# Two weight pieces loaded before the last table third, three converted before chunk 0, and most of a gate offset moved from products to transfers

## The chip, the core and the metric

The kernel runs on one core of one Trainium2 chip. TensorE (PE) multiplies, VectorE (DVE), ScalarE (ACT) and GpSimd (POOL) do the elementwise work, and SyncE (SP) issues nearly all transfers; each engine runs its own instructions in order. The metric is the device time of one execution in microseconds, the median of several runs.

## The reference

The input x has 8 batches of 3008 points with 256 features. It is transformed along both axes, the real part is kept, and every resulting row goes through a gated layer.

```python
X = np.fft.fft(np.fft.fft(x, axis=1), axis=2).real      # (8, 3008, 256)
x = X.reshape(24064, 256)
gate = 1.0 / (1.0 + np.exp(-(x @ w_gate)))              # w_gate, w_val: 256 x 1536
val = x @ w_val
out = gate * val @ w_out                                # w_out: 1536 x 256
```

The weights come in as 64-bit floats and are used as 32-bit ones.

## The kernel before

**Transform.** The points of a batch are folded on their symmetry, and the sums over points are matrix products with a table of cosines and one of sines (`stab`). Batch 0 is brought in by three thirds of x (`load_third`) and three thirds of each table (`load_table(t, j)`, two transfers each; t = 0 cosines, t = 1 sines). The results are `pk` (cosine side) and `qk` (sine side). The transform over features is merged into the weights: `merge` multiplies a converted piece of w_gate or w_val with the small table `dt`, and `merged` (ACT, L349) copies the result from PSUM into `G`. `G1` goes with pk, `G2` with qk.

**Weights.** There are 18 pieces (`jobs`): 0 to 11 are pieces of w_gate and w_val in turn, each for two column tiles f; 12 to 17 are pieces of w_out. A piece is loaded by SP (`weight_load`, 512 KB), split by two ACT activations (`weight_parts`, L301 and L302), put together by three DVE steps by way of a PSUM bank (`weight_join`, L313 to L316), and finished by an addition on POOL (L318). Then PE merges it (`weight_use`, tile name `ps`). Pieces 0 to 7 go through all this in the prologue, the others around the first steps of the main loop. The table of jobs and steps (`pre`, `mid`, `use`) says at which step i a piece's parts, join and use are placed.

**The offset ge.** One feature has no partner on the sine side. Its row `ek` times a number per column tile is written into PSUM ahead of the products, by `seed(i)` on ACT (L660, two activations with the scale `ge[:, g, f]`). `ge` is the first row of `G2`, turned so that each of 128 numbers lies on its own partition. `ge_sums` turns it on PE: a product of one row of G2 with a single 1.0 out of the tile `busy` for each column tile, and `ge_out` (ACT, L365) copies the column out of PSUM.

**Main loop.** A chunk is 252 output points. For every chunk the 12 column tiles f follow one another, one per step i. In a step PE does `front_a(i)` (G1 by pk, on top of the seed), then whatever weight work and products with the hidden layer are due, then `front_b(i)` (G2 by qk). Between the two, ACT keeps twice the first half (`part`, L671). One step later `gate_a` and `gate_b` make the gated values (ACT L685 and L699; DVE L686, L698 and L702). `seed(i + 1)` is given to ACT in step i, so column tile 4 is needed in step 3, tile 6 in step 5. From step 5 on, `back` multiplies the hidden layer with w_out: for the first chunk directly (`rows_start`, tile name `rows`), later by a scheme with fewer products (`po`).

**Banks.** Three PSUM banks (tag `x`) hold merges of the prologue and the seeded tiles `pf`. Five others (tags `po0` to `po4`) hold the sums of the sequence products, the joins and the ge products, and later the output sums.

**Order.** Each engine's order is the order of the calls. On SP, after the loads of pieces 0 to 7, x and the cosine table, come the three thirds of the sine table, pieces 8 to 13, then (when x is done with) pieces 14 to 17, the store of er to `ed`, and in the loop the rows `ek`, the mirror copies of later batches (`xr`) and the outputs. An SP transfer is not issued before the one eight places ahead of it has landed. The last sines (`sines(2)`) need the last third of the sine table.

Of the kernel before, what the change touches and what calls it, by code (L numbers as in the profile page):

```python
# [82 lines left out]
def kernel(  # L83
# [10 lines left out]
    nc = tc.nc  # L94
    B, _, _, _, D = xf.shape
    F = moe_w_gate.shape[1]
    P = 128
# [9 lines left out]
    NB = 1 + max(b // 3 for b in PLACE)  # L107
# [3 lines left out]
    N3 = NQ // 2  # L111
# [25 lines left out]
    def bank(name, other=None):  # L137
        if other is not None:
            return pso.tile([P, 512], F32, name=name, tag=f"po{other}")
        return psx.tile([P, 512], F32, name=name, tag="x")  # L140
# [45 lines left out]
    G1, G2 = G[:, 0], G[:, 1]  # L186
    ge = const.tile([P, 2, NFT], F32, name="ge")
# [8 lines left out]
    def load_table(t, j):  # L196
        q = slice(2 * j, 2 * j + 2)
        for rows in (slice(0, 112), slice(112, NP)):
            nc.sync.dma_start(out=ST[0][rows, t, q], in_=stab[rows, t, q])
# [48 lines left out]
    KEEP = 14  # L248

    def weight_load(j):  # L250


        w, c = jobs[j]
        src = (moe_w_gate, moe_w_val, moe_w_out)[w]
        src = src[2 * c * P : 2 * (c + 1) * P, :] if w == 2 else src[:, c * WC : (c + 1) * WC]
        src = src.rearrange("(c p) f -> p c f", p=P)

        def some(n, pool, tag):

            if tag not in shared:  # L260
                shared[tag] = pool.tile([P, n * WC], F32, name=f"w{tag}", tag=tag)
            return shared[tag]

        def home(j):

            if j in (0, 1, 2, 9):
                t = hp.tile([P, 6 * WC], F32, name="raw", tag="h")
                return t[:, 0 : 4 * WC], t[:, 4 * WC :]
            if j in (3, 4):
                ws = some(5, pqp, "qk")[:, (j - 3) * 2 * WC : (j - 2) * 2 * WC]  # L270
                return sp.tile([P, 4 * WC], F32, name="raw", tag="sf"), ws
            if j < 9:
                t = wf[:, (j - 4) % 4].rearrange("p m n -> p (m n)")
                return t[:, 0 : 4 * WC], t[:, 4 * WC : 6 * WC]
            if j < 12:
                shared[j] = cp.tile([P, 10 * WC], F32, name="wc", tag="c")
                return shared[j][:, 0 : 4 * WC], shared[j][:, 4 * WC : 6 * WC]
            return (shared[10][:, 6 * WC :] if j == 12 else shared["qk"][:, 0 : 4 * WC],
                    shared[11][:, (6 + 2 * (j - 12)) * WC : (8 + 2 * (j - 12)) * WC])

        if j < KEEP:
            raw, ws = home(j)
        else:
            both = some(24, xp, "x4").rearrange("p (i n) -> p i n", n=2 * WC)
            i = 3 * (j - KEEP)
            raw, ws = both[:, i : i + 2].rearrange("p a n -> p (a n)"), both[:, i + 2]
        raw = raw.bitcast(I32).rearrange("p (c f w) -> p c f w", c=2, w=2)
        ws = ws.rearrange("p (c f) -> p c f", c=2)
        WS[j] = ws
        if src.dtype == F32:  # L290
            nc.sync.dma_start(out=ws, in_=src)
        else:
            RAW[j] = raw
            nc.sync.dma_start(out=raw.rearrange("p c f w -> p c (f w)"), in_=src.bitcast(I32))  # L294

    def weight_parts(j):

        if j in RAW:
            raw, ws = RAW[j], WS[j]
            lo, hi = raw[:, :, :, 0], raw[:, :, :, 1]  # L300
            nc.scalar.activation(ws, hi.bitcast(F32), AF.Abs)  # L301
            nc.scalar.activation(lo, lo.bitcast(U32), AF.Copy, scale=2.0 ** -29)  # L302

    def weight_join(j, other=None):
        if j not in RAW:
            return
        raw, ws = RAW.pop(j), WS[j]
        lo, hi = raw[:, :, :, 0], raw[:, :, :, 1]
        wi = ws.bitcast(I32)
        mid_ = ws if other is None else bank("join", other).rearrange("p (c f) -> p c f", c=2)  # L310
        mi = mid_.bitcast(I32)
        ts = nc.vector.tensor_scalar
        ts(out=mid_, in0=ws, scalar1=2.0 ** -15, scalar2=HUGE, op0=ALU.max, op1=ALU.min)  # L313
        ts(out=mi, in0=mi, scalar1=3, scalar2=0x3FFFFFF8, op0=ALU.logical_shift_left,
           op1=ALU.bitwise_and)
        nc.vector.scalar_tensor_tensor(out=wi, in0=hi, scalar=-(2 ** 30), in1=mi,  # L316
                                       op0=ALU.bitwise_and, op1=ALU.bitwise_or)
        nc.gpsimd.tensor_tensor(wi, wi, lo, op=ALU.add)  # L318
# [25 lines left out]
    def merged(j):  # L344

        g, c = jobs[j]
        ps = MERGED.pop((g, c))
        cs = slice(c * WC, (c + 1) * WC)
        nc.scalar.copy(G[:, :, g, cs], ps.rearrange("p (h n) -> p h n", h=2))  # L349

    def ge_at(js):
        return [(jobs[j][0], f) for j in js for f in range(2 * jobs[j][1], 2 * jobs[j][1] + 2)]

    def ge_sums(js, other, ps=None):

        ps = bank("ge", other) if ps is None else ps
        for g, f in ge_at(js):
            mm(ps[:, g * NFT + f : g * NFT + f + 1], G2[0:1, g, f * P : (f + 1) * P], busy[0:1, 0:1],
               True, True)
        return ps  # L360

    def ge_out(js, ps):
        gs, fs = [sorted({a[i] for a in ge_at(js)}) for i in range(2)]
        to = slice(gs[0], gs[-1] + 1), slice(fs[0], fs[-1] + 1)
        nc.scalar.copy(ge[:, to[0], to[1]],  # L365
                       ps[:, 0 : 2 * NFT].rearrange("p (g f) -> p g f", g=2)[:, to[0], to[1]])
# [286 lines left out]
    def seed(i):  # L653

        _, _, n, f, _ = cut(i)
        PF[i] = bank("pf").rearrange("p (g n) -> p g n", g=2)[:, :, 0:n]
        for g in range(2):
            nc.scalar.activation(PF[i][:, g], EK[i // NFT], AF.Copy, scale=ge[:, g, f : f + 1])  # L660

    def front_a(i):
        (pk, *_), ks, _, _, fs = cut(i)
        for g in range(2):
            mm(PF[i][:, g], G1[:, g, fs], pk[:, ks], False, True)

    def part(i):

        pqe, ks, n, f, _ = cut(i)
        AP[i] = app.tile([P, 2, CH], F32, name="ae", tag="ae")[:, :, 0:n]  # L670
        nc.scalar.activation(AP[i], PF[i], AF.Copy, scale=2.0)  # L671
# [222 lines left out]
    ges = None  # L894
    for j in range(8):
        weight_parts(j)
        if j > 2:
            merged(j - 3)
        weight_join(j, j % 3)
        if j == 7:  # L900
            merged(5)
            ge_sums((4, 5), None, ges)
        weight_use(j)
        if 2 < j < 7:
            ges = ge_sums((j - 3,), 3, ges)
    ge_out(range(6), ges)
    for j in (6, 7):
        merged(j)
    for j in range(N3):
        load_table(1, j)  # L910
    for j in range(8, KEEP):
        weight_load(j)
    seq_start(0)
    folds = fold_ops(0, 2)
# [12 lines left out]
        for f in put:  # L927
            f(high)
    e0_spread()
    for i in range(N3):  # L930
        seed(i)
    for j in (8, 9):
        weight_parts(j)
    weight_join(8, NB - 1)
    sin = [seq_group(0, blk, 1, (2 * blk, 2 * blk + 1)) for blk in range(2)]

    def sines(j):
        for sums, _, _ in sin:
            sums(2 * j, 2 * j + 1)

    def first(i):
        front_a(i)
        if i < 2:
            part(i)
    sines(0)
    first(0)
    sines(1)
    first(1)
    sines(2)
    first(2)  # L950
    put = [then() for _, then, _ in sin]
    for high in range(2):
        for f in put:
            f(high)
    weight_join(9, NB - 1)
    for j in range(KEEP, len(jobs)):
        weight_load(j)
    nc.sync.dma_start(out=ed[0:1], in_=shared["er"])
    weight_parts(10)

    per = NFT * len(chunks)
    side = {}
# [5 lines left out]
    pre, use, mid = {}, {}, {}  # L968
    def using(j):
        weight_use(j, j % 2)  # L970
        if jobs[j][0] < 2:
            merged(j)
    for j, i in ((8, -2), (9, -1), (10, 0), (11, 1), (12, 2), (13, 4), (14, 6), (15, 8), (16, 10), (17, 12)):
        if i > 0:
            pre.setdefault(i - 1, []).append(lambda j=j: weight_parts(j))
        if i >= 0:
            mid.setdefault(i, []).append(lambda j=j: weight_join(j, 2))
        if jobs[j][0] == 2:
            use.setdefault(i + 2, []).append(lambda j=j: using(j))
    for j, i, other in ((8, 0, 3), (9, 2, 4), (10, 3, 3), (11, 4, 0)):  # L980
        use.setdefault(i, []).append(lambda j=j: using(j))
        use.setdefault(i + 1, []).append(lambda j=j, other=other: ge_out((j,), ge_sums((j,), other)))
    use[0].append(lambda: ge_out((6, 7), ge_sums((6, 7), 4)))


    i0 = NFT
# [123 lines left out]
```

## Time and profile before

| | us |
|---|---|
| median of 3 runs (lowest, highest) | 1935.59 (1934.75, 1937.33) |
| the profiled execution | 1937.33 |
| its span, first to last instruction | 1935.5 |
| PE busy | 1924.0 |
| POOL, DVE, ACT busy | 1561.6, 1435.0, 1346.7 |
| last sines on PE | 47.39 to 49.92 |
| first product of the hidden layer (rows) | 74.06 |
| ge products on PE (tile ge), before 39.7 and after 54.86 | 3.30 and 3.67 |

How to read it: the span is what the trace covers, and the time of an execution is 1.8 us more. Busy times of engines overlap. The mean granted clock of TensorE over the span is 0.998 of full speed. The stretch that the change touches ends at about 74 us; the rest of the span repeats chunks in which PE is busy nearly all the time.

### The profile page before, as it was taken

The numbers are of one execution on the slowest core, as the hardware profiler recorded it, in microseconds if no ns is written. First come the engines' busy times: TensorE is split into PE (matmuls) and PEld (weight loads), VectorE is DVE, ScalarE is ACT, GpSimd is POOL, SyncE is SP. The second block draws the span as 40 slices with busy tenths as digits, with TensorE's granted clock in tenths as the row PEclk, the third lists the DMA queues.
The fourth block names the chain that finished last, engine by engine and source line by source line (L and its number), as shares of the span: only waits on it lengthen the run. The fifth ranks groups of instructions, "written<-read, shape, count | busy, mean of one in ns | idle before, by whom it ended". The sixth has DMA issues, their size and how long they took to land.

```text
span 1935.5 us, 34483 instructions
## 1 busy us (share of the span) xinstructions
PE 1924.0 (99%) x11292; PEld 1793.3 (93%) x11292; DVE 1435.0 (74%) x3210; ACT 1346.7 (70%) x3152; POOL 1561.6 (81%) x2806
## 2 busy tenths in 40 slices
PE   9999999999999999999999999999999999999999
PEld 6899989999999999999999999999999999999998
DVE  7647887787777877777777776777777777776776
ACT  4777757767777677776777767777677766777775
POOL 2389988997889788987889879888789886777775
PEclk9999999999999999999999999999999999999999
DMA  9351421202022211312112021111200110011111
GB/s 289 124 111 36 107 79 47 58 17 79 15 56 51 63 31 20 77 24 80 19 42 60 14 83 24 47 47 24 83 14 15 22 20 14 15 20 22 25 17 30
DMA packets 165098, 97.87 MB, mean 51 GB/s; under 512 B 126298, under 2 KB 155068, under 8 KB 163128
## 3 DMA queue, kind: packets, MB, share of 16 engines
q1 hardware_dynamic: 164366, 95.17, 20.5%
q8 instruction: 91, 1.49, 0.3%
q14 instruction: 87, 0.71, 0.1%
q10 hardware_dynamic: 522, 0.50, 0.1%
q0 software_dynamic: 32, 0.00, 0.0%
HBM read 70.40 MB, written 47.24 MB: 61 GB/s over the span
## 4 chain that ended last, share of the span: by engine, by line
PE 94%; DVE 2%; DMA 2%; ACT 1%; SPq 0%; issue 0%; ACTq 0%; DVEq 0%
PE pf L135 49%; PE po L135 40%; PE ev L135 2%; PE rows L135 1%; DMA st<-in_stab_dram 1%; DVE c L826 1%; DMA raw<-in_moe_w_val_dram 1%; PE od L135 1%; DMA wf<-in_moe_w_val_dram 1%; DVE z L686 0%; PE ps L135 0%; PE row L135 0%; ACT pf L699 0%; DVE h L702 0%; DVE h L698 0%; SPq L294 0%
## 5 line engine op out<-in xcount | busy, mean ns | idle before, releaser
L708 POOL TENSOR_TENSOR sf<-h 128x168 f32<-128x168 f32 (+1 forms) x935 | 517.1, 572 | 215.9 <-DVE h L702 215.8
L708 POOL TENSOR_TENSOR sf<-h,sf 128x168 f32<-128x168 f32 (+1 forms) x1122 | 622.6, 574 | 57.5 <-DVE h L702 57.0
L135 PE MATMUL pf<-qk,G 128*128 128x252 f32 (+1 forms) x2304 | 584.3, 376 | 1.9 <-ACT ae L671 1.9
L135 PE MATMUL pf<-pk,G 128*128 128x252 f32 (+1 forms) x2304 | 582.9, 376 | 0.0
L702 DVE TENSOR_TENSOR h<-pf,z 128x252 f32<-128x252 f32 (+1 forms) x576 | 241.7, 420 | 425.7 <-ACT pf L699 425.7
L660 ACT ACTIVATE pf<-ek,ge 128x252 f32<-128x252 f32 (+1 forms) x1152 | 542.6, 471 | 19.3 <-DVE h L702 0.4
L135 PE MATMUL po<-sf,wf 128*128 128x168 f32 (+1 forms) x2992 | 516.2, 305 | 0.0
L671 ACT ACTIVATE ae<-pf 128x504 f32<-128x504 f32 (+1 forms) x576 | 339.0, 589 | 234.0 <-PE pf L135 231.8
L135 PEld LDWEIGHTS pf<-pk,G 128*128 128x128 f32 x2304 | 436.4, 190 | 53.3 <-issue 1.6
L135 PEld LDWEIGHTS po<-sf,wf 128*128 128x128 f32 x2992 | 460.5, 190 | 8.1
L135 PE MATMUL po<-h,wf 128*128 128x168 f32 (+1 forms) x2618 | 463.3, 305 | 0.0
L826 DVE TENSOR_TENSOR c<-c 128x168 f32<-128x168 f32 (+1 forms) x929 | 440.2, 506 | 5.1
L135 PEld LDWEIGHTS pf<-qk,G 128*128 128x128 f32 x2304 | 411.4, 190 | 29.7 <-ACT ae L671 3.1
L135 PEld LDWEIGHTS po<-h,wf 128*128 128x128 f32 x2618 | 416.5, 190 | 16.2
L686 DVE TENSOR_TENSOR z<-ae,pf 128x504 f32<-128x504 f32 (+1 forms) x576 | 383.7, 666 | 35.9 <-ACT h L685 34.4
L685 ACT ACTIVATE h<-pf 128x252 f32<-128x252 f32 (+1 forms) x576 | 217.7, 378 | 163.6 <-PE pf L135 158.2
L699 ACT ACTIVATE pf<-z 128x252 f32<-128x252 f32 (+1 forms) x576 | 214.0, 372 | 87.6 <-DVE h L698 85.2
L698 DVE TENSOR_TENSOR h<-h,pf 128x252 f32<-128x252 f32 (+1 forms) x576 | 233.0, 405 | 0.0
L708 POOL TENSOR_TENSOR sf<-sf 128x168 f32<-128x168 f32 (+1 forms) x187 | 107.2, 573 | 14.7
L708 POOL TENSOR_TENSOR sf<-sf,h 128x168 f32<-128x168 f32 (+1 forms) x187 | 101.7, 544 | 0.0
L739 ACT COPY c<-po 128x504 f32<-128x504 f32 (+1 forms) x141 | 80.0, 568 | 0.0
L835 DVE STREAM_TRANSPOSE os<-c 128x256 f32<-128x256 f32 x184 | 70.6, 421 | 0.3 <-issue 0.3
(152 smaller groups left out, 917.5 us busy)
## 6 DMA issues: line engine op xcount, KB each, us to landing
x<-xr SPq DMA_DIRECT2D x14, 1536.0 KB
out_dram<-os SPq DMA_DIRECT2D x368, 56.0 KB
xr<-in_xf_dram SPq DMA_DIRECT2D x14, 768.0 KB
xr<-in_xf_dram SPq DMA_DIRECT2D x35, 256.0 KB
ek<-ed SPq DMA_DIRECT2D x39, 126.0 KB
out_dram<-os SPq DMA_DIRECT2D x284, 7.0 KB
st<-in_stab_dram SPq DMA_DIRECT2D x6, 658.9 KB
x<-in_xf_dram SPq DMA_DIRECT2D x3, 1024.0 KB
```

The source lines that it names most:

```text
L135: nc.tensor.matmul(o, l, r, start=start, stop=stop, skip_group_check=True)
L660: nc.scalar.activation(PF[i][:, g], EK[i // NFT], AF.Copy, scale=ge[:, g, f : f + 1])
L671: nc.scalar.activation(AP[i], PF[i], AF.Copy, scale=2.0)
L685: nc.scalar.activation(H[p][:, fh, 0:n], PF[i][:, 0], AF.Sigmoid)
L686: nc.vector.tensor_tensor(z[:, :, ::-1], AP.pop(i), PF[i], op=ALU.subtract)
L698: nc.vector.tensor_tensor(h[:, fh, 0:n], h[:, fh, 0:n], pf[:, 1], op=ALU.mult)
L699: nc.scalar.activation(pf[:, 0], z[:, 0], AF.Sigmoid)
L702: nc.vector.tensor_tensor(h[:, fh, n:], pf[:, 0], z[:, 1], op=ALU.mult)
L708: nc.gpsimd.tensor_tensor(block(p, dst), block(p, a), block(p, b), op=(ALU.subtract, ALU.add)[op])
L739: (nc.vector.tensor_copy if t == 1 or t == 3 and not last else nc.scalar.copy)(C[0][:, 3 * t * R : 3 * (t + 1) * R], PO[t][:, 0 : 3 * R])
L826: engine.tensor_tensor(t[:, dst * R : (dst + 1) * R], *v, op=(ALU.subtract, ALU.add)[op])
L835: nc.vector.transpose(os_[0][:, s, 0:nb, h, :], t[:, c0 : c0 + nb * TB])
```

## The change

Four things are done.

1. SP loads pieces 8 and 9 ahead of the last third of the sine table, not behind it.
2. Pieces 8, 9 and 10 are split and joined before the last part of the sequence products is copied out: 8 and 9 between seed(0) and seed(1), 10 after the first sines and seed(2). Before, piece 8 was joined there and piece 9 just ahead of the loop. All three use bank po4. Piece 11 is split ahead of the loop and joined in step 0; before, this was piece 10, and 11 came in step 1.
3. Pieces 8, 9, 10 and 11 are merged in steps 0, 1, 2 and 3; before, in steps 0, 2, 3 and 4.
4. ge is made by products for pieces 0 to 3 alone. For pieces 4 to 11 each column tile is brought from G2's first row to the 128 partitions of ge by a transfer on SP (`ge_load`): 512 bytes each, two for a piece. The eight for pieces 4 to 7 stand behind the loads of pieces 14 to 17 and ahead of the store of er; the two for each of pieces 8 to 11 follow its merge. The copy of merge 5 into G moves behind merge 7.

```diff
+    def ge_load(j):
+        for g, f in ge_at((j,)):
+            nc.sync.dma_start(out=ge[:, g, f : f + 1], in_=G2[0:1, g, f * P : (f + 1) * P])
+
...
         weight_join(j, j % 3)
-        if j == 7:
-            merged(5)
-            ge_sums((4, 5), None, ges)
         weight_use(j)
-        if 2 < j < 7:
+        if j > 2 and j < 7:
             ges = ge_sums((j - 3,), 3, ges)
-    ge_out(range(6), ges)
-    for j in (6, 7):
+    ge_out(range(4), ges)
+    for j in (5, 6, 7):
         merged(j)
     for j in range(N3):
+        if j == N3 - 1:
+            weight_load(8)
+            weight_load(9)
         load_table(1, j)
-    for j in range(8, KEEP):
+    for j in range(10, KEEP):
         weight_load(j)
...
-    for i in range(N3):
-        seed(i)
+    seed(0)
     for j in (8, 9):
         weight_parts(j)
-    weight_join(8, NB - 1)
+        weight_join(j, NB - 1)
+    seed(1)
     sin = [seq_group(0, blk, 1, (2 * blk, 2 * blk + 1)) for blk in range(2)]
...
-    def first(i):
-        front_a(i)
-        if i < 2:
-            part(i)
-    sines(0)
-    first(0)
-    sines(1)
-    first(1)
-    sines(2)
-    first(2)
+    for j in range(N3):
+        sines(j)
+        front_a(j)
+        if j < 2:
+            part(j)
+        if not j:
+            seed(2)
+            weight_parts(10)
+            weight_join(10, NB - 1)
     put = [then() for _, then, _ in sin]
     for high in range(2):
         for f in put:
             f(high)
-    weight_join(9, NB - 1)
     for j in range(KEEP, len(jobs)):
         weight_load(j)
+    for j in range(4, 8):
+        ge_load(j)
     nc.sync.dma_start(out=ed[0:1], in_=shared["er"])
-    weight_parts(10)
+    weight_parts(11)
...
-    for j, i in ((8, -2), (9, -1), (10, 0), (11, 1), (12, 2), (13, 4), (14, 6), (15, 8), (16, 10), (17, 12)):
+    for j, i in ((11, 0), (12, 2), (13, 4), (14, 6), (15, 8), (16, 10), (17, 12)):
         if i > 0:
             pre.setdefault(i - 1, []).append(lambda j=j: weight_parts(j))
-        if i >= 0:
-            mid.setdefault(i, []).append(lambda j=j: weight_join(j, 2))
+        mid.setdefault(i, []).append(lambda j=j: weight_join(j, 2))
         if jobs[j][0] == 2:
             use.setdefault(i + 2, []).append(lambda j=j: using(j))
-    for j, i, other in ((8, 0, 3), (9, 2, 4), (10, 3, 3), (11, 4, 0)):
-        use.setdefault(i, []).append(lambda j=j: using(j))
-        use.setdefault(i + 1, []).append(lambda j=j, other=other: ge_out((j,), ge_sums((j,), other)))
-    use[0].append(lambda: ge_out((6, 7), ge_sums((6, 7), 4)))
+    for j in range(8, 12):
+        use.setdefault(j - 8, []).append(lambda j=j: (using(j), ge_load(j)))
```

## The prediction

> **What bounds the kernel now.** I read the busy times and the chain of waits on the page first, then the busy time by stage, the chain of the first 160 us, and the SyncE queue (SP).
>
> ```profile
> PE 1924.0 (99%) x11292; PEld 1793.3 (93%) x11292; DVE 1435.0 (74%) x3210; ACT 1346.7 (70%) x3152; POOL 1561.6 (81%) x2806
> ...
> PE 94%; DVE 2%; DMA 2%; ACT 1%; SPq 0%; issue 0%; ACTq 0%; DVEq 0%
> ```
>
> TensorE (PE) sets the end. The stages say where it is not at its best (columns: stretch, its length, then busy time and count on PE, PEld, DVE, ACT, POOL; granted clock, DMA share, GB/s):
>
> ```profile
> 39.70:50.92 11.22, 10.67 (x37) 6.64 (x36) 3.92 (x8) 7.28 (x16) 1.16 (x1) 1.00 1.02 307
> 53.10:57.06 3.96, 2.19 (x14) 1.81 (x14) 3.58 (x6) 0.90 (x3) 1.33 (x2) 1.00 1.05 393
> 57.06:63.80 6.74, 6.74 (x18) 5.52 (x19) 5.87 (x11) 4.55 (x11) 2.50 (x2) 0.50 0.08 28
> 74.06:1923.60 1849.54, 1847.53 (x10967) 1737.68 (x10967) 1375.48 (x3101) 1304.55 (x3066) 1537.89 (x2780) 1.00 0.19 43
> ```
>
> After 74 us PE idles 2 us in 1849, so a microsecond won or lost on PE's path before 74 us reaches the end whole. In 57.06:63.80 the granted clock is 0.50: the work took 6.74 us where full clock would take 3.37. It follows a stretch in which PE was busy 2.19 of 3.96 us, half of it single-column products. The chain names this work:
>
> ```profile
> 54.12 0.70 DVE raw L316
> 54.83 0.04 issue
> 54.87 1.05 PE ge L135 x8
> 55.91 1.05 PE pf L135 x4
> 56.96 0.81 PE ge L135 x4
> 57.78 1.98 PE pf L135 x4
> 59.76 3.41 PE ps L135 x8
> 63.17 2.12 PE pf L135 x8
> 65.29 0.53 PE ge L135 x4
> 65.82 1.92 PE ps L135 x8
> 67.74 1.70 PE pf L135 x8
> ```
>
> PE stood still until 54.87 for the last DVE step (L316) of converting piece 9, because ge (6, 7) shares its PSUM bank. Then ge lies between the products: 1.05 us for two pieces, 0.53 for one (two more follow, 69.44 and 73.60). Front products pf cost 0.85 a pair (1.70 for two), a merge (ps) 1.92.
>
> **Part 1: ge leaves PE.** After the last sines the loop loses ge for pieces 6 and 7 (1.05) and 8, 9, 10, 11 (4 x 0.53): 3.17 us at full clock. ge for 4 and 5, two pieces, leaves the prologue; there PE waits for DVE's folds and for the x transfer that ends DVE's wait at 32.02, so I take 0. The five small ACT copies (0.15 each) are off the path.
>
> **Part 2: the wait and the clock.** Nothing in chunk 0 shares a bank with a late conversion: the wait 53.10 to 54.87, 1.77 us, goes. Merge 8 started at 51.10, waiting for POOL; front_a(2) had ended about 50.77, so 0.33 goes. If the idle stretch goes, so should the half clock behind it: 6.74 - 3.37 = 3.37 us. Gains: 3.17 + 1.77 + 0.33 + 3.37 = 8.64.
>
> [...]
>
> **Part 3: two pieces ahead of the last table third.** ACT's conversions of 8 and 9 began as they landed:
>
> ```profile
> 46.78 0.67 ACT L301 ACTIVATE wf<-wf 128x512 f32<-128x512 f32 x1 [3.63 <-DMA wf<-in_moe_w_gate_dram]
> 48.20 0.68 ACT L301 ACTIVATE raw<-raw 128x512 f32<-128x512 f32 x1 [0.18 <-DMA raw<-in_moe_w_val_dram]
> ```
>
> So with the last table third ahead of them both were down by 48.2. Changed order, same bytes: that third lands by about 48.2, at most 48.9 (the second third had landed by 42.5, when the eighth issue behind it went out; 3.7 us for a third, two pieces of 1.35). Its sines ran from 47.39 without a wait; they now start between 48.2 and 48.9: +0.8 to +1.5, I take +1.1. ACT does parts 8, 9 ahead of seed(1), which ends near 47.4, so front_a(1) ends near 48.3, inside the same wait.
>
> The conversions cost nothing: DVE idles from 41.56 to 47.48 and takes joins 8 and 9 (three steps of 0.72) there. Piece 10 lands near 49.5 as before; ACT's parts(10) (1.25) precede part(1) and the two copies of the sines, DVE's join(10) (to about 52.4) precedes the first qk sums, done by 53.4. PE has front_a(2) from 51.0 and merge 8 from 51.9 to 53.8 as cover; without cover front_b(0) would wait at most 0.7. Join 11 (2.15) precedes gate_a(0) on DVE, and that cover holds too: front_a(3) at 61.0 needs seed(3) by 60; it can run at 58.4.
>
> Merges 9, 10, 11 now come one per step, i = 1, 2, 3, so step 4 has nothing between front_a(4) and front_b(4). part(4) on ACT took 0.59 after PE's matmuls had ended: PE idles 0.85 there. Costs: 1.1 + 0.85 = 1.95.
>
> **Part 4: sixteen small transfers on SP.** The first eight go behind pieces 14 to 17 and ahead of er's store; the rest follow merges 8 to 11, ahead of and behind chunk 1's ek row, all ahead of the mirror copies. Nothing among these is due before 80 us. What decides is when pieces 4 and 5 land: seed(4) needs them by 62.8 (front_a(4) at 63.8), seed(6) needs 6 and 7 by 68.8. SP reaches the first at about 53.3 (its last four loads were issued from 50.12 in 1.90 us, now 1.1 later). No transfer of 128 four-byte pieces into 128 partitions is in the trace. The neighbours:
>
> ```profile
> L649 SPq DMA_DIRECT2D ek<-ed x47: 338/344/2576, 74.2 to 1857.2; - x47
> ...
> L593 SPq DMA_DIRECT2D x<-in_xf_dram x7: 830/2146/9371, 103.6 to 136.1; - x7
> ...
> SPq L649 <- DMA ed<-er: 5.6, 1, 5.6
> ```
>
> Lower bound: ek's issue, 128 rows, 0.34 us. Upper bound: x8's (L593), 11.8 KB in 4-byte pieces, 3024 of them, 0.83 to 9.37. With 128 pieces ge is nearest ek: I take 0.4, four issued by 55, eight by 56.5 but for SP's waits for the transfer eight places back (a piece of a load each, the last landing near 59.5). The er store, issued at 52.12 at the end of the same queue of loads, landed 5.6 us after its issue, at 58.0; ge for 4 and 5 should land by 59 to 60, for 6 and 7 by 62. Both have room: 0.
>
> [...]
>
> **Sum.** 8.64 - 1.95 = 6.7 us. The profiled execution took 1937.33, its span 1935.5: the span should come to 1928.8 and that execution to 1930.6. The median of three, 1.74 below the profiled one, becomes 1935.59 - 6.7 = 1928.9. Stages that won't be shorter: DVE was busy 17.93 us between 50.92 and 74.06 and loses two joins (4.3), 13.6 left for a stage of some 16.4, so it doesn't become the bound.
>
> **Rivals.**
> A, the forecast: 1928.9, between 1927.0 (no cost at all, 8.64) and 1931 (waits for qk and the table at their upper bounds, 0.7 + 0.4, and a microsecond of unseen waits).
> B, the half clock stays or comes at another place: PE stands still for 1.1 us ahead of the last sines, and a gap of 1.77 was enough before. For it: one gap of like size did it. Against: around 41 us PE idled 0.55 us (two waits seen by PEld, 1.2) without a fall, and behind the new gap dense matmuls follow. It gives back 3.37: 1935.59 - 3.3 = 1932.3.
> C, ge's issue is as slow as x8's median, 2.15: the fourth lands at 53.3 + 8.6 + 0.5 = 62.4, just in time; the eighth at 71.0 for 68.8, so 2.2 are lost: 1931.1. Against: x8 has 24 times the pieces.
> D, the other side: SP serves the scattered transfers as it did x8's on average, (0.94 + 5.16 + 15.13) / 7 = 3.03 us. The fourth lands at 65.9, 3.1 late; the eighth at 78.0, when seed(6) would be due at 71.9: 6.1 more. PE stands idle in front_a(4) and front_a(6), which brings the half clock (3.37): -6.7 + 9.2 + 3.4 = +5.9, 1941.5. From 2.7 us an issue on it is slower without the clock (53.8 + 8 x 2.7 = 75.4, 6.6 past 68.8), from 2.3 with it. For it: elements of four bytes; against: their number.
> E, nothing reaches the end: some wait of chunk 0 that the present waits hide, such as ACT or DVE chains from seed to seed, takes all: 1935.6. Against: the stage's DVE and ACT have 2 us and more to spare.
>
> **How the numbers follow.** A 0.64, B 0.12, C 0.10, D 0.11, E 0.03. About 0.2% (3.9 us) can be told from no change: faster is A, C and a quarter of B, 0.77; same the rest of B and E, 0.12; slower D, 0.11. The range takes A, B, C: 1926.5 (the no-cost bound less half a microsecond of spread) to 1933.5 (B and a microsecond), with 0.86.
>
> **What would show it.** No ge on PE after 30 us; granted clock 1.00 from 10 to 1900 us; the last sines starting at 48.2 to 48.9 behind a wait for the table; merges 8 to 11 within 52 to 63; the first rows product at about 67.2 instead of 74.06; ACT's seeds (L660) with no wait for a DMA. The forecast is wrong if seed(4) or seed(6) waits for ge's transfers, if the sines wait beyond 49, if the clock shows 0.5 between 47 and 67, or if PE idles by more than 3 us in all between 51 and 68.

## The result, and the profile after

| | before | after |
|---|---|---|
| median of 18 runs each (lowest, highest) | 1935.66 (1934.05, 1938.08) | 1931.72 (1928.27, 1933.60) |
| ratio, 95% interval | | 0.9977 (0.997 to 0.9984) |
| the profiled execution | 1937.33 | 1931.39 |
| its span | 1935.5 | 1929.5 |
| start of front_a(2) on PE | 49.92 | 50.85 |
| first product of the hidden layer (rows) | 74.06 | 68.25 |
| from there to the end of the span | 1861.4 | 1861.25 |

The kernel became 3.9 us faster by the medians (3.1 to 5.8 by the interval); 6.7 had been forecast. The last line says where to look: once the rows products begin, both kernels take the same time, so all is decided ahead of it, in the first 74 us.

Busy times and the chain of waits on the page of the changed kernel:

```profile
PE 1916.0 (99%) x11260; PEld 1786.7 (93%) x11260; DVE 1433.5 (74%) x3210; ACT 1346.7 (70%) x3147; POOL 1562.0 (81%) x2806
...
PE 94%; DVE 3%; DMA 2%; ACT 1%; issue 0%; SPq 0%; ACTq 0%; DVEq 0%
```

PE has 32 matmuls fewer (16 pairs of ge) and 8.0 us less to do, of which 3.37 had been half clock. The same by stage (stretch, its length, busy time and count on PE, PEld, DVE, ACT, POOL, granted clock, DMA share, GB/s):

```profile
38.89:50.85 11.96, 9.94 (x34) 6.00 (x33) 6.86 (x12) 7.99 (x17) 2.58 (x2) 1.00 1.04 299
50.85:68.25 17.40, 15.26 (x69) 12.59 (x68) 13.21 (x25) 13.24 (x30) 3.88 (x3) 1.00 0.49 140
68.25:1918.00 1849.75, 1847.74 (x10969) 1737.81 (x10968) 1376.20 (x3106) 1305.93 (x3066) 1539.61 (x2781) 1.00 0.19 43
```

The stretch from front_a(2) to the first rows shrank from 24.14 (49.92 to 74.06) to 17.40 us, at full clock throughout; PE still idles 17.40 - 15.26 = 2.14 us in it. The stretch of the sequence products ahead of it has 2.02 us of idle PE (11.96 - 9.94) where before's had 0.55. PE's timeline of the changed kernel shows both (start, length, instruction; in brackets the idle time just before it and what ended it):

```profile
47.36 1.12 PE L135 MATMUL pf<-pk,G 128*128 128x252 f32 x4 [1.47 <-ACT pf L664]
48.31 0.80 PE L135 MATMUL ev<-st,x 126*128 126x377 f32 x2
...
50.85 1.01 PE L135 MATMUL pf<-pk,G 128*128 128x252 f32 x4
51.70 1.89 PE L135 MATMUL ps<-wf,dt 128*128 128x256 f32 x8
53.43 1.01 PE L135 MATMUL pf<-qk,G 128*128 128x252 f32 x4
...
60.17 1.12 PE L135 MATMUL pf<-pk,G 128*128 128x252 f32 x4 [0.57 <-ACT pf L664]
...
66.42 1.12 PE L135 MATMUL pf<-qk,G 128*128 128x252 f32 x4 [1.56 <-ACT ae L675]
67.38 1.04 PE L135 MATMUL pf<-pk,G 128*128 128x252 f32 x4
```

Behind 47 us three waits are left, all for ACT: front_a(1) for seed(1) (1.47), front_a(3) for seed(3) (0.57), front_b(4) for part(4) (1.56); the other 0.55 ahead of 50.85, for DVE, was there before too. 0.57 + 1.56 = 2.13 is all of the idle time behind 50.85. ACT's timeline says why (seed, part and the sigmoids stand in lines L664, L675 and L689 of the changed kernel):

```profile
45.21 0.67 ACT L301 ACTIVATE raw<-raw 128x512 f32<-128x512 f32 x1 [1.56 <-DMA raw<-in_moe_w_val_dram]
45.79 0.66 ACT L302 ACTIVATE raw<-raw 128x512 int32<-128x512 uint32 x1
46.34 0.97 ACT L664 ACTIVATE pf<-ek,ge 128x252 f32<-128x252 f32 x2
...
63.94 0.66 ACT L301 ACTIVATE wc<-wqk 128x512 f32<-128x512 f32 x1
64.51 0.64 ACT L302 ACTIVATE wqk<-wqk 128x512 int32<-128x512 uint32 x1
65.05 0.56 ACT L349 COPY G<-ps 128x512 f32<-128x512 f32 x1
65.51 0.38 ACT L689 ACTIVATE h<-pf 128x252 f32<-128x252 f32 x1
65.79 0.58 ACT L675 ACTIVATE ae<-pf 128x504 f32<-128x504 f32 x1
```

seed(1) (46.34) is queued behind the split of piece 9, which waited for its load. part(4) (65.79) is queued behind the split of piece 13, the copy of merge 11 and a sigmoid of gate 3: it starts 1.2 us after PE's four products from 63.74 (about 0.85 of work) have ended, where I had counted on its own 0.59 alone.

The chain of work that ended last holds no PE between 49.8 and 66.4 us. It runs through DVE and ACT: joins 10, 11 and 12, the splits of pieces 12 and 13 and the gates are its main links. The part around join 12 and seed(4) (start, length, engine, what):

```profile
60.28 0.62 DVE join L313
60.90 0.02 issue
60.92 0.71 DVE join L314
61.63 0.02 issue
61.66 0.69 DVE wc L316
62.34 0.34 DVE h L706
62.69 0.02 issue
62.71 0.48 ACT pf L664
```

So chunk 0 is now set by the order of DVE's and ACT's work, though each of the two is busy only 13.2 of its 17.40 us.

SP's timeline, and its group of ge transfers (least, median and greatest time of one issue in ns):

```profile
53.05 7.64 SPq L364 DMA_DIRECT2D ge<-G  x8
60.79 0.40 SPq L962 DMA_DIRECT2D ed<-er  x1
61.28 2.42 SPq L364 DMA_DIRECT2D ge<-G  x4
...
L364 SPq DMA_DIRECT2D ge<-G x16: 469/548/612, 53.0 to 66.2; - x16
```

A ge transfer took 0.55 us to issue (0.4 assumed); the first eight were out by 60.7, with 3.0 us of that spent in three waits for loads eight places back. No seed waited for a transfer: the waits of L664 are two, both for DVE, 1.1 us in all.

### The profile page after: what moved, and what is told of

The parts are those of the page before. It is cut to its first block, busy times and chain, and to the rows that moved or that the text cites. A ratio compares the mean times of both kernels' runs of the same rounds, so it can differ in the third digit from the quotient of the medians.

```text
span 1929.5 us, 34456 instructions
## 1 busy us (share of the span) xinstructions
PE 1916.0 (99%) x11260; PEld 1786.7 (93%) x11260; DVE 1433.5 (74%) x3210; ACT 1346.7 (70%) x3147; POOL 1562.0 (81%) x2806
## 4 chain that ended last, share of the span: by engine, by line
PE 94%; DVE 3%; DMA 2%; ACT 1%; issue 0%; SPq 0%; ACTq 0%; DVEq 0%
PE pf L135 49%; PE po L135 40%; PE ev L135 2%; DMA st<-in_stab_dram 2%; PE rows L135 1%; DVE c L830 1%; DMA wc<-in_moe_w_gate_dram 1%; PE od L135 1%; DVE z L690 0%; ACT pf L703 0%; PE row L135 0%; DMA raw<-in_moe_w_val_dram 0%; DVE h L706 0%; DVE h L702 0%; ACT ae L675 0%
## 5 line engine op out<-in xcount | busy, mean ns | idle before, releaser
L664 ACT ACTIVATE pf<-ek,ge 128x252 f32<-128x252 f32 (+1 forms) x1152 | 543.0, 471 | 20.0 <-DVE h L706 1.1
L675 ACT ACTIVATE ae<-pf 128x504 f32<-128x504 f32 (+1 forms) x576 | 339.6, 590 | 232.5 <-PE pf L135 229.3
L689 ACT ACTIVATE h<-pf 128x252 f32<-128x252 f32 (+1 forms) x576 | 218.1, 379 | 161.6 <-PE pf L135 156.9
```

The source lines that it names most:

```text
L689: nc.scalar.activation(H[p][:, fh, 0:n], PF[i][:, 0], AF.Sigmoid)
```

## Experiments

Twelve runs, in sessions of up to four on one chip. "Before" is the median of the kernel before in the same session.

| | edit | median | before | ratio (95%) |
|---|---|---|---|---|
| b_again | before, again | 1936.05 | 1935.78 | 1.0 (0.9991 to 1.0009) |
| a_again | after, again | 1930.25 | 1935.78 | 0.9969 (0.9956 to 0.9981) |
| b_fill | before + dense products where PE waits | 1935.39 | 1935.78 | 0.9997 (0.9988 to 1.0005) |
| b_ge | before + ge transfers alone | 1931.86 | 1935.78 | 0.9978 (0.9968 to 0.9987) |
| a_prod | after, ge of 4 to 11 by products | 1934.85 | 1935.55 | 0.9995 (0.9986 to 1.0004) |
| a_seeds | after, seeds first on ACT | 1932.55 | 1935.55 | 0.9982 (0.9973 to 0.9991) |
| a_late13 | after, piece 13 a step later | 1931.33 | 1935.55 | 0.9977 (0.9968 to 0.9986) |
| a_both | the two edits above | 1931.09 | 1935.55 | 0.9978 (0.997 to 0.9987) |
| c_load | after, seeds first, old order of loads | 1932.33 | 1936.36 | 0.9981 (0.9972 to 0.9989) |
| c_cand | the same, pieces placed anew | 1932.77 | 1936.36 | 0.9983 (0.9974 to 0.9992) |
| a_again2 | after, third time | 1930.66 | 1935.62 | 0.9974 (0.9963 to 0.9985) |
| a_late13_2 | a_late13 again | 1930.78 | 1935.62 | 0.9971 (0.9961 to 0.9982) |

**b_again: the kernel before, unchanged**, for a second trace of it.

> The kernel before once more, for a second trace of it and its spread. Theory (the 3.37 us of half clock were in the profiled execution and not in every one): ratio 1.000, and a span 1 to 3 us under 1935.5 with a shorter half-clock stretch or none. Rival (half clock is in every execution and the shortfall lies in the changed kernel alone): again 6 to 7 us at 0.50 behind the wait for piece 9, span 1935 or more.

In this execution there was no half clock. PE's timeline of it:

```profile
53.19 1.05 PE L135 MATMUL ge<-busy,G 1*128 1x1 f32 x8 [1.16 <-DVE raw L316]
...
60.58 1.12 PE L135 MATMUL pf<-pk,G 128*128 128x252 f32 x4 [1.13 <-ACT pf L660]
```

The wait for the bank is there, 1.16 instead of 1.77. The second line is new: at full clock PE comes to front_a(3) before ACT has written seed(3). In the first profile the half clock covered this wait. From front_a(2) to rows it took 21.28 us (49.29 to 70.57) against 24.14: 2.86 less, of which 0.61 is the shorter wait for the bank and 3.37 - 1.13 = 2.24 what the half clock cost net, by these two traces.

The runs of the kernel before in all sessions here, this one included, give the size: of 102 whose granted clock was listed, 62 had a mean clock of 0.998 or less and took 1936.65 us on average, 40 had 0.999 or more and took 1934.71. I read the lower mean clock as the half clock of the first trace: 3.37 us lost in 1935.5 make a mean of 0.998. It is then in some six of ten executions and costs 1.9 us there, so 62 / 102 x 1.94 = 1.2 on average. Where in an execution the clock fell is seen in the traces alone.

**a_again: the changed kernel, unchanged.**

> The changed kernel once more. Theory (its cost is the order of ACT's work, the same in each execution): waits of PE again at front_a(1) (1.5 us), front_a(3) (0.6) and front_b(4) (1.6), span within 1 us of 1929.5, 3 to 5 us under the kernel before. Rival (landing of transfers varies and sets the time): other waits, at the sines or at the seeds for a DMA, and a span that moves by 2 us or more with them.

The same three waits: 1.42, 0.67 and 1.56; 17.49 us from front_a(2) to rows. The span, 1930.8, is 1.3 longer than the first one, and the gain in the time, 5.5, is more than was expected; PE also waited 1.62 for a third of the cosine table here, so the rival is right in part. This and a_again2 have 12 runs, all at a clock of 0.999 or more, and of the 18 runs of the result one is at 0.998 (the slowest, 1933.60): the half clock of the old place did not come back.

**b_fill: does the idle stretch cause the half clock?** Four dense products, whose result nothing uses, stand in the kernel before where PE waits for the bank.

```diff
+    def fill(n):
+        ps = bank("fill", 1)
+        for _ in range(n):
+            mm(ps[:, 0:CH], busy[:, 0:P], busy, True, True)
+    use[0].append(lambda: fill(4))
```

> The kernel before, with four dense products into a free bank where PE waits for piece 9's conversion (their output is not used). Theory (the idle and thin stretch lets the clock fall): the clock stays at 1.00 from 57 to 64 us and the time falls by what the half clock costs on average, 1.5 to 3.4 us. Rival (the clock falls for another reason, or seldom): no change within 1 us, or slower by up to 1.7 us if the fill itself is in the way.

All 11 runs had a mean clock of 1.000, against 40 of 102 at 0.999 or more without the fill. PE by stage from front_a(2) on, first the kernel with the fill, then b_again over the like stretch:

```profile
49.38:53.40 4.02, 4.02 (x20) 3.58 (x19) 3.62 (x7) 3.36 (x7) 0.56 (x1) 1.00 0.73 218
```

```profile
49.29:53.19 3.90, 2.74 (x13) 2.09 (x12) 3.50 (x7) 2.90 (x6) 0.00 (x0) 1.00 0.83 253
```

PE is busy all of 4.02 us, where it was busy 2.74 of 3.90. So the idle stretch is the cause here, and with dense work in it none of the 11 runs shows the fall. The time did not fall by the 1.5 to 3.4 that the theory named (1935.39; the interval takes in no change): the ge products came 0.56 later (53.75 against 53.19), seed(3) was waited for as before (1.13), and 1.2 us was all there was to win on average; 0.56 of it went to the fill itself.

**b_ge: the ge transfers (the fourth item of the change) alone.** The kernel before with ge of pieces 4 to 11 by transfers, its order of loads and conversions kept.

```diff
-        if j == 7:
-            merged(5)
-            ge_sums((4, 5), None, ges)
...
+    for j in range(4, 8):
+        ge_load(j)
...
-    for j, i, other in ((8, 0, 3), (9, 2, 4), (10, 3, 3), (11, 4, 0)):
-        use.setdefault(i, []).append(lambda j=j: using(j))
-        use.setdefault(i + 1, []).append(lambda j=j, other=other: ge_out((j,), ge_sums((j,), other)))
-    use[0].append(lambda: ge_out((6, 7), ge_sums((6, 7), 4)))
+    for j, i in ((8, 0), (9, 2), (10, 3), (11, 4)):
+        use.setdefault(i, []).append(lambda j=j: (using(j), ge_load(j)))
```

> The kernel before with ge of pieces 4 to 11 by transfers and nothing else changed: loads, conversions and merges stay in the old order. Theory (ge's products, the wait for the shared bank and the clock are the gain, the new order of loads and conversions costs): 5 to 7 us under the kernel before, so 1 to 3 under the changed one. Rival (the new order is what pays, or the transfers cost on SP): 3 us or less under the kernel before.

It gained 3.9 us, less than expected and as much as the whole change in the result. What the first three items bring on top can hardly be seen: 0.8 us by the means (1931.88 over 9 runs, 1931.06 over the 30 of the changed kernel), with an uncertainty as large; beside it on the same chip, a_again's five runs were 1.6 us faster by the medians. PE's timeline and a window of it:

```profile
55.43 1.99 PE L135 MATMUL ps<-raw,dt 128*128 128x256 f32 x8 [0.97 <-POOL raw L318]
60.31 1.80 PE L135 MATMUL pf<-pk,G 128*128 128x252 f32 x4 [1.99 <-ACT pf L664]
```

```profile
60.00:63.00 3.00, 2.69 (x7) 2.23 (x8) 2.93 (x6) 2.22 (x6) 0.98 (x2) 0.60 0.18 34
```

Without the ge products the wait for the bank is gone, but two others took its place: merge 9 waits for POOL's last step of piece 9 (0.97), front_a(3) for seed(3) (1.99), and behind that the clock falls to 0.60 over 60 to 63. DVE, busy 2.93 of these 3 us, had joins 9 to 12 in this stage.

**a_prod: the order alone.** The changed kernel with ge of pieces 4 to 11 made by products again, on banks po3 and po4, so that none shares one with a late conversion.

```diff
-    for j in range(4, 8):
-        ge_load(j)
...
-        use.setdefault(j - 8, []).append(lambda j=j: (using(j), ge_load(j)))
+        use.setdefault(j - 8, []).append(lambda j=j: using(j))
+    for j, other in ((8, 3), (9, 4), (10, 3), (11, 4)):
+        use.setdefault(j - 7, []).append(lambda j=j, other=other: ge_out((j,), ge_sums((j,), other)))
+    use[0].append(lambda: ge_out((6, 7), ge_sums((6, 7), 4)))
```

> The changed kernel with ge of pieces 4 to 11 by products again (banks po3 and po4 in turn, each one step after its merge); loads, conversions and merges in the new order. Theory (the transfers carry the gain, the new order alone little): 2 to 3.5 us slower than the changed kernel, 1 to 2 under the kernel before. Rival (the new order carries the gain): within 1 us of the changed kernel.

It is 0.7 us faster than before, which can't be told from nothing, and some 3.4 slower than the changed kernel (1934.85 against a pooled median of 1931.4). From front_a(2) to rows, by stage:

```profile
52.46:71.35 18.89, 18.74 (x94) 15.45 (x92) 13.75 (x26) 13.83 (x35) 3.89 (x3) 1.00 0.33 119
```

PE is full: 18.74 us of 18.89, against 15.26 with the transfers, and 18.74 - 15.26 = 3.48 is what the ge products cost (3.17 in the sum). The stretch is 2.4 us shorter than in b_again, but it starts at 52.46, 3.2 later: in these traces, what the order wins behind the sines it gives back ahead of them. With the ge products on it PE, idle for 0.15 us of that stretch, sets chunk 0; without them it is idle for 2.14, for ACT, and the chain runs through DVE and ACT.

**a_seeds: who makes front_a(1) late?** The changed kernel with the three seeds ahead of the splits of pieces 8 and 9 on ACT.

```diff
-    seed(0)
+    for i in range(N3):
+        seed(i)
     for j in (8, 9):
         weight_parts(j)
         weight_join(j, NB - 1)
-    seed(1)
```

> The changed kernel with the three seeds ahead of the conversions on ACT, as before the change. Theory (PE's 1.5 us wait ahead of front_a(1) is ACT's order: seed(1) behind piece 9's landing and split): front_a(1) without a wait, the last sines waiting for the table instead by 0 to 1, 0.5 to 1.5 us faster than the changed kernel. Rival (the table lands no earlier than seed(1) is ready): the same wait of 1.5 us moves to the last sines, no change in time.

The wait of front_a(1) went, and the time did not follow. PE's timeline, and its window behind:

```profile
48.57 0.92 PE L135 MATMUL ev<-st,x 126*128 126x377 f32 x2 [2.68 <-DMA st<-in_stab_dram]
```

```profile
48.00:52.00 4.00, 3.43 (x7) 2.03 (x8) 2.02 (x4) 2.05 (x4) 1.28 (x1) 0.66 0.47 173
```

Between 36 us and front_a(2) PE now waits once, for the last table third (2.68), and the clock falls to 0.66 behind it. The rival was right: here the table is the later of the two, and seed(1) only stood in front of it. Piece 10, next in the queue behind the table, landed 1.0 us after it (49.60 against 48.57). In the profile of the changed kernel piece 10 was there at 49.11, which puts the table at about 48.1 as an estimate, 0.2 ahead of the last sines: without the wait for seed(1) they would hardly have started sooner.

**a_late13: part(4) behind piece 13.** The changed kernel with piece 13 split in step 4 and joined in step 5.

```diff
-    for j, i in ((11, 0), (12, 2), (13, 4), (14, 6), (15, 8), (16, 10), (17, 12)):
+    for j, i in ((11, 0), (12, 2), (13, 5), (14, 6), (15, 8), (16, 10), (17, 12)):
```

> The changed kernel with piece 13 split, joined and used one step later (step 5 in place of 4). Theory (front_b(4) waits 1.6 us because part(4) stands behind piece 13's two activations on ACT): that wait falls to 0.7, 0.7 to 1 us faster than the changed kernel. Rival (part(4) waits for the gates of step 3, on DVE): no change.

PE's timeline:

```profile
63.03 1.12 PE L135 MATMUL pf<-qk,G 128*128 128x252 f32 x4 [0.68 <-ACT ae L675]
```

The wait fell from 1.56 to 0.68, and front_a(2) to rows from 17.40 to 16.56. In the time, 1931.33, nothing shows: 0.9 us is less than what front_a(2)'s start moves from trace to trace (48.30 here, 50.85 in the first).

**a_both: the two edits together.**

> Seeds first and piece 13 a step later in one kernel. Theory (two separate waits on PE's path): the gains add, 1.2 to 2.5 us faster than the changed kernel, 5.5 to 7 under the kernel before. Rival (the second wait takes up what the first gives): no more than the better of the two alone.

A miss: the chunk took 16.68 us, with the 0.68 again, but the median is 1931.09, no better than piece 13's move alone. In its profiled execution PE stood still earlier, for a third of the cosine table, which the change does not touch:

```profile
37.41 0.81 PE L135 MATMUL pe<-st,x 126*1 126x377 f32 x8 [3.34 <-DMA st<-in_stab_dram]
```

**c_load: does the new order of loads earn anything?** a_seeds with pieces 8 and 9 loaded behind the last table third again.

```diff
-        if j == N3 - 1:
-            weight_load(8)
-            weight_load(9)
         load_table(1, j)
-    for j in range(10, KEEP):
+    for j in range(8, KEEP):
```

> The changed kernel with seeds first and pieces 8 and 9 loaded behind the last table third, as before the change; conversions still all ahead of the sine sums' copies. Theory (the new load order costs about 2 us at the last sines, but the early conversions need it): front_a(2) starts near 49.7 as in the kernel before, the qk sums come about 2 us later behind joins 9 and 10, front_b(0) waits 1 to 2 us, and the time is within 1 us of the changed kernel. Rival (the load order costs without need): 1.5 us or more faster than the changed kernel.

PE's timeline:

```profile
54.29 1.12 PE L135 MATMUL pf<-qk,G 128*128 128x252 f32 x4 [1.19 <-DVE qk L537]
```

front_a(2) starts at 49.84, early as expected, but the joins now stand on DVE ahead of the qk sums, and front_b(0) waits 1.19 for them; rows begin at 69.60. Against the kernel before of its own session c_load gains 4.0 us and a_seeds 3.0: the two orders are worth the same within about a microsecond.

**c_cand: the old order of loads, with the pieces placed to fit.** Loads and seeds are as in c_load; the edit, in part:

```diff
...
+            weight_parts(8 + j)
+            weight_join(8 + j, NB - 1)
...
-    for j, i in ((11, 0), (12, 2), (13, 4), (14, 6), (15, 8), (16, 10), (17, 12)):
+    for j, i in ((10, 0), (12, 2), (11, 4), (13, 5), (14, 6), (15, 8), (16, 10), (17, 12)):
...
-    for j in range(8, 12):
-        use.setdefault(j - 8, []).append(lambda j=j: (using(j), ge_load(j)))
+    for j, i in ((8, 0), (9, 1), (10, 2), (11, 6)):
+        use.setdefault(i, []).append(lambda j=j: (using(j), ge_load(j)))
```

> Old load order, seeds first, pieces 8 and 9 converted as they land ahead of the qk sums, joins 10, 12, 11, 13 in steps 0, 2, 4, 5 and merges 8, 9, 10, 11 in steps 0, 1, 2, 6 (pieces 10 and 11 are due at step 9), ge by transfers as in the changed kernel. Theory (the table's delay and ACT's and DVE's queues at steps 3 and 4 are what the change gave back): front_a(2) near 49.7, the stretch from there to the first rows product 15.5 to 16.5 with one merge moved behind it, 1 to 2 us faster than the changed kernel. Rival (the landing of pieces 8 and 9 now holds the qk sums): no faster than the changed kernel.

A miss. Chunk 0 took 17.08 us, and merge 11, now behind the first rows, comes on top (1.73). PE waited for part(3) (0.74), seed(4) (0.60) and part(4) (1.08), probably because, with merge 11 out of step 3, PE comes sooner to where ACT is late; this was not tried alone. Five of 11 runs were at a clock of 0.998, and no trace shows where it fell in them.

**a_again2 and a_late13_2**, side by side on one chip, to see whether piece 13's place counts.

> The changed kernel a third time, beside the next one on the same chip. Theory: 3.5 to 5 us under the kernel before; the granted clock of nearly all executions 0.999 or 1.000. Rival (the half clock comes back with the new waits): a third or more of the executions at 0.998 or less.

> The changed kernel with piece 13 a step later, a second time, since its trace showed 0.9 us less between front_a(2) and the first rows product and its median did not. Theory (the 0.9 reaches the end): 0.5 to 1.3 us faster than the changed kernel. Rival (landing of the loads hides it or it is too small to be seen): within 0.4 us of it.

1930.66 and 1930.78. Over all their runs (30 and 18) the means are 1931.06 and 1931.01: no difference, though with this spread one of less than about 0.9 can't be seen, so whether piece 13's 0.9 reaches the end stays open. No version tried can be told to beat the changed kernel.

## Why the prediction was right in sign and too large

**ge's products (3.17): right.** a_prod puts them at 3.48 in PE's busy time and 3.4 in the time. b_ge gains 3.9 by removing them together with the wait for the bank and mostly with the half clock (8 of its 9 runs are at a clock of 0.999 or more). That ge of pieces 4 and 5 is worth nothing in the prologue agrees with it too: front_a(0) starts at 43.26 in b_ge, at 43.16, 42.52 and 42.61 in the three traces with these products.

**SP's transfers hidden: right.** 0.55 us an issue, and 7.64 us for the first eight with waits; in the profile after, the seeds waited for DVE alone (1.1 us). Rivals C and D needed 2.15 and 3.03 an issue. The eighth of those transfers had landed by 65.0, 12 us after the first was issued: then SP issued the one eight places behind it (so too in the chain of the first profile: the 24th transfer went out at 35.14, once the 16th had landed at 35.12).

**The wait for the bank (1.77): right in kind, somewhat large.** It is gone in every trace of the changed kernel; b_again has it at 1.16. The 0.33 ahead of merge 8 belonged to the one execution: b_again has no such wait.

**The half clock (6.74 - 3.37 = 3.37): the step that failed.** The mechanism was right: b_fill shows that the idle stretch made the clock fall (1.000 in all 11 runs with the stretch filled), and the changed kernel does not have the fall (29 of its 30 runs at 0.999 or more). The term was sized as if each execution had it and as if all of it lay on the path. It comes in 62 of 102 executions, and where it comes it costs 1.9 by the runs, 2.24 by the two traces, because it covers front_a(3)'s wait for seed(3): 1.2 on average. Put in place of 3.37, it turns 6.7 into 4.5; pooled, the change measured 4.4 by medians (1935.8 over 102 runs, 1931.4 over 30) and 4.8 by means. That this comes so close is luck in part, as the other terms show. The profiled execution of before, 1937.33, lay 1.7 above its median, and I subtracted from the median a saving found in that execution. Against that execution itself the forecast was 1930.6, and the profiled execution after took 1931.39.

**The rest of the sum, at full clock: 8.64 - 3.37 - 1.95 = 3.3.** The runs of before at a clock of 0.999 or more took 1934.71 on average, and the 29 of the changed kernel's 30 runs at such a clock took 1930.97: 3.74 less. The size is right; the parts are not quite. From front_a(2) to rows, b_again's idle PE is 21.28 - 18.95 = 2.33 us and after's 2.14, so hardly any idle time was removed there: the work fell by 3.7 (18.95 to 15.26), and the waits of 1.16 and 1.13 were replaced by 0.57 and 1.56. By these traces the chunk is 3.88 shorter (21.28 to 17.40) and starts 1.2 later: 2.7 of the 3.74. The other microsecond was not located; the starts move by more than that from trace to trace. The prediction's reason why DVE could not become the bound, 13.6 us of work in a stage of 16.4, missed what the chain above shows: the sum of DVE's work fits, but its steps and ACT's wait for each other.

**The wait at step 4 (0.85): mis-sized.** It was 1.56, because part(4) is queued behind three other kinds of ACT work that I had not counted; a_late13 shows that piece 13's split is 0.88 of it. With 0.57 at front_a(3), this is 1.28 more than forecast, and the rows began at 68.25, not 67.2.

**The later sines (1.1): right by the changed kernel's three traces, with a spread that was not foreseen.** They started at 48.31 (48.2 to 48.9 forecast), though not behind a wait of their own: front_a(1) ahead of them had stood 1.47 for seed(1), which I had put inside the wait for the table; a_seeds shows the table close behind it. front_a(2) starts at 50.85, 51.79 and 49.65 in the three traces of the changed kernel (mean 50.8), at 49.92 and 49.29 in the two of before (49.6): 1.2 later. Over all eight traces with the new order of loads it starts at 48.3 to 53.7 (mean 51.5), over the six with the old one at 48.3 to 50.0 (mean 49.5): 2.1 later, about twice the forecast.

**The rivals.** B (the half clock stays, 1932.3) comes close in time but not in cause: the clock held 1.00 from 10 to 72 us in the profile after. A fall behind another wait of PE, which B supposed, is seen in b_ge and a_seeds. E was wrong for the whole change, but half right for the order of the loads, whose worth some waits of ACT, DVE and the table do take: it named chains of ACT and DVE from seed to seed, and those are what sets chunk 0 in the profile after.

## What to carry to other kernels

A throttled clock seen in one profiled execution is to be counted over many before it is put into a sum (here 62 of 102 had it), and what other engines would be late with at full clock is to be taken off it (here 1.13 of 3.37 us). Where an instruction is to follow its producer at once, all that is queued ahead of it on the in-order engine counts, not its own duration alone: part(4) began 1.2 us after the products it follows, behind a split, a copy and a sigmoid. Tiny products that cost little and share a bank with a late conversion can be worth taking off the matmul engine altogether, if another queue has room: here 3.48 us of PE's work went for sixteen issues of 0.55 us on SP, and most of this change's worth lay there. When the engine that sets the end is relieved, the chain through the others has to be followed link by link; their busy shares alone (13.2 of 17.40 us for each here) do not show that they will take over.

## What was not expected of the hardware

- **A short idle stretch was followed by half clock in one execution and not in another.** 1.77 us of idle PE and thin products around it were followed by 6.74 us at 0.50; the same program, with 1.16, kept 1.00 in another execution. Behind a single wait of 2.68 us (a_seeds) the loss was 4 x 0.34 + 4 x 0.08 = 1.7 us over 48 to 56, some 3.4 us at half clock; behind 3.34 us (a_both) it was 4.5 x 0.38 = 1.7 us over 37.5 to 42. Yet waits of 1.86 (a_prod) and 2.06 us (a_late13_2) left the clock at 1.00 (over 34 to 76 us and 38 to 70 us), so the length alone does not decide; what does stays open.
- **Loads landed at different times in each execution.** PE's wait for the same third of the cosine table went from none (a_late13) to 3.34 us (a_both), that for seed(1) behind piece 9's load 0.17 (a_again2) or 2.06 (a_late13_2), with nothing changed ahead of them. From the first rows product to the end of the span every trace but c_cand's, which has a merge behind it, takes 1861.2 to 1861.8 us, so the executions differ ahead of it. At a clock of 0.999 or more the changed kernel's runs span 5.1 us (standard deviation 1.5), those of before 2.4 (0.7), and with the old order of loads c_load has 1.0 where a_seeds has 1.7. This agrees with a path that now leans on such a load; that the loads alone make this spread was not tried.
